# Rests of the MLP's first operands, joins of weight words and a third chunk of w_out, moved in an attention and MLP kernel

## The chip, the cores and the metric

One core of a Trainium2 chip runs the whole program. The metric is the device time of one execution in microseconds, as the median of several runs. The engines are named as in the profile: PE (TensorE), DVE (VectorE), ACT (ScalarE), POOL (GpSimd), and SP (SyncE), whose queue issues all the DMAs here.

## The reference

```python
def _attn_ref(q, k, v):                      # q, k, v: (8, 12, 448, 64), float32
    scores = scale * np.matmul(q, k.transpose(0, 1, 3, 2)) - np.log(S)
    attn = 1.0 / (1.0 + np.exp(-scores))
    return np.matmul(attn, v).astype(np.float32)

def _moe_ref(x, w_in, w_out):                # x: (3584, 768); w_in: (768, 2048); w_out: (2048, 768), both float64
    h = x @ w_in
    r = np.maximum(h, 0.0)
    return ((r * r) @ w_out).astype(np.float32)
```

The attention is a sigmoid attention (no sum over keys). Its output, with the heads side by side, is the x of a two-layer MLP whose activation is the squared Relu.

## The kernel before

**Two kinds of stage.** The first stage (0 to 262 us of the span) does the attention of all 48 pairs of heads; eight stages follow, a first and a second MLP product for each of four groups of two batches. A matmul in the needed accuracy is three: an operand is split into a high part (a cast to fp32r) and a rest, its low part (the operand minus the high part), and high x high, high x low and low x high are summed. Each MLP product is made from seven half-size products (numbers 1 to 7) over sums and differences of blocks, so the operands of x and the blocks of the weights have to be added up first.

**A block of the attention stage.** `block(d)` (line 422) handles two pairs, n = 2d and n + 1, and 24 blocks run in an order written out by hand. On PE: the scores of both pairs (L269), the rest of their keys (L285), then attention times v (`attn_v`, L306, 24 matmuls in one piece), whose sums lie in a PSUM tile `duo` of which there is one. The second pair's scores need that tile again, so `put` (L315, two copies by DVE) must have emptied it before they start. On ACT: seven sigmoids, then the first step of the words below. On DVE, in this order: a piece of weight work, the cast `high` of a coming q, k pair (L472), the two copies of `put`, the rest `low` of that pair (L476); then, behind the issue of the scores, another piece of weight work, `high` and `low`. I call these the first and the second half of a period.

**Weights.** The weights come as float64. While the attention runs, 14 of their 16 chunks are made ready: two loads of a chunk's words (`load_chunk`), a first step by ACT (`convert_words`, L145 and L146), a second by three DVE instructions and an addition by POOL (`convert_join`, L150 to L157), then four additions by DVE (`sums`, L166 to L169) and two stores. These are numbered k = 3j + h for chunk j: k = 3j + 1 and 3j + 2 are joins, k = 3j + 3 the sums. `weights_of` (line 484) puts number k into half period `k * NWP // NK`. The chunks in `DEFERRED`, two of w_out, are made ready in the first MLP stage instead, by `deferred(i, at)` (line 178), in four quarters with their loads, words, joins, sums and stores at steps counted from `at`. That stage (`gemm1` for group 0, 56 steps of 9 matmuls) and all later ones but for the tails of the first MLP stages of groups 1 to 3 are put in order by the framework's planner, which gives earlier code the higher priority.

**Pieces.** Behind the blocks named in `PIECES` (line 65) the operands of the first MLP stage are made from the attention's first output: numbers 1, 2, 3 and 6 are each three casts on ACT and three rests on DVE (`make`, `split_to`, L325 and L326), t1 to t3 are three subtractions on DVE (L351).

**In the first MLP product,** `run(n, i)` (line 547) issues step (n, i): nine matmuls, then a copy of a PSUM bank by ACT (`snap`) or an addition out of it by DVE, and `squares` for each second i (L539 on ACT for the block "12", L541 on DVE for the others).

Of the kernel before, what the change touches and what calls it, by code (L numbers as in the profile page):

```python
# [8 lines left out]
F32 = mybir.dt.float32  # L9
# [26 lines left out]

NWP = 45

# [23 lines left out]

DEFERRED = (6, 7)

PIECES = {13: (1,), 15: (2,), 17: ("t1",), 19: (3,), 21: ("t2",), 22: (6,), 23: ("t3",)}


@with_exitstack
def sigmoid_attention_relu2_mlp(
# [250 lines left out]

    def split_to(hi, lo, raw, vector=False):
        if vector:
            nc.vector.tensor_copy(out=hi, in_=raw)
        else:
            nc.scalar.copy(out=hi, in_=raw)  # L325
        nc.vector.tensor_sub(out=lo, in0=raw, in1=hi.bitcast(F32))  # L326

# [5 lines left out]
    def x_operands(g):  # L333
# [20 lines left out]

        def make(product, n, vector=False):
            h2, l2 = (op2(f"x{n}_{g}{c}", F32R) for c in "hl")
            if g == 0 and product in (1, 2, 3, 6):
                both = op2(f"y{n}_{g}", F32R)
                h1, l1 = both[:, 0], both[:, 1]
            else:  # L360
                h1, l1 = (op1(f"y{n}_{g}{c}", F32R) for c in "hl")
            ops[product] = [(h2[:, 0], l2[:, 0]), (h2[:, 1], l2[:, 1]), (h1, l1)]
            parts = ops[product] if g == 0 else [(h2, l2), (h1, l1)]
            for x, (hi, lo) in zip(raw[n], parts):
                split_to(hi, lo, x, vector)

# [6 lines left out]
        return ops, {  # L373
            1: lambda vector=False: make(1, "11", vector),
            2: lambda vector=False: make(2, "21", vector),
            "t1": lambda: sub("t1", "12", "11"),
            "t2": lambda: sub("t2", "22", "t1"),
            6: lambda: make(6, "t2"),
            "t3": lambda: sub("t3", "t2", "11"),
            7: lambda: make(7, "t3"),  # L380
            5: lambda: make(5, "t1"),
            3: lambda: make(3, "22"),
            "t4": lambda: sub("t4", "21", "t2"),
# [9 lines left out]
    x, vt, xs, at, pav, f64, w, rest = {}, {}, {}, {}, {}, {}, {}, {}  # L393
    ready, stores = [], []
    pieces = {}
    ops = {}

    def half(j, h):
        return w[j][0].rearrange("p a n -> p (a n)")[:, (DM, 0)[h] : (2 * DM, DM)[h]]

    def weights_join(k):


        j, h = divmod(k, 3)
        if h == 0 and j > 0:
            ready.append(sums(*todo[j - 1], *w[j - 1]))
        elif h > 0:
            convert_join(f64[j, h - 1], half(j, h - 1))
        if h < 2 and j + 1 < len(todo):
            f64[j + 1, h] = load_chunk(*todo[j + 1], h)  # L410

    def weights_words(k):

        j, h = divmod(k, 3)
        if j < len(todo) and h < 2:
            if h == 0:
                w[j] = wide(f"a_{j}"), wide(f"s_{j}")
            convert_words(f64[j, h], half(j, h))

    NK = 3 * len(todo) + 1  # L420

    def block(d):
# [12 lines left out]
        if d == 0:  # L435
            for m in (1, 2, 3):
                high(m)
                low(m)
            score(0, (x[0],), ((0, 0),))
            rest[0] = scores_rest(0, (x[0], x[1]))  # L440
        else:
            weights_of(weights_join, n - 1)
            high(n + 3)
            put(n - 2)
            put(n - 1)
            low(n + 3)
            score(n, xs[n])
        score(n + 1, xs[n + 1])
        if more:
            rest[d + 1] = scores_rest(d + 1, (x[n + 2], x[n + 3]))  # L450
        pav[n], pav[n + 1] = attn_v_rest(d, rest.pop(d), vt[d])
        weights_of(weights_join, n)
        high(n + 4)
        low(n + 4)
        weights_of(weights_words, n)
        weights_of(weights_words, n + 1)
        if more:
# [4 lines left out]
        attn_v(n + 1, pav[n + 1], at[n + 1], vt[d])  # L462
        pieces_of(*PIECES.get(d, ()))

# [56 lines left out]
    def gemm1(g, ops, weights, between):  # L521
# [12 lines left out]
        def squares(n, i, scalar=False):  # L534
            if i % 2 == 0:
                return
            t = blocks[n, i // 2]
            if scalar:
                nc.scalar.activation(t, t, AF.Square)  # L539
            else:  # L540
                nc.vector.scalar_tensor_tensor(out=t, in0=t, scalar=0.0, in1=t, op0=ALU.max, op1=ALU.mult)  # L541

        def snap(k, i):
            s = snaps[k, i] = op1(f"s{k}_{g}_{i}")
            nc.scalar.copy(out=s, in_=banks["a", i])  # L545

        def run(n, i):
            if n in (1, 5) and (i, n == 5) not in weights:
                weights[i, n == 5] = halve_weights(load_first(i, n == 5, g))
# [20 lines left out]
            elif n == 5:  # L570
                snap(4, i)
                nc.vector.tensor_add(out=tile_of("22", i), in0=banks["b", i], in1=snaps[4, i])
                squares("22", i)
            elif n == 3:
# [5 lines left out]
            elif n == 4:  # L580
                nc.vector.tensor_add(out=tile_of("21", i), in0=out, in1=snaps[2, i])  # L581
                squares("21", i)

# [26 lines left out]
        with ExitStack() as fixed:  # L610
            if g > 0:
                fixed.enter_context(tc.manual_schedule())
            for at, (n, i) in enumerate(tail):
# [3 lines left out]
                for behind, piece, arg in (*work, (5, load, 1), (8, halve, 1)):  # L617
                    if behind == at:
                        piece(arg)
        return blocks, operands, second  # L620

# [89 lines left out]
    with tc.manual_schedule():  # L711
        with tc.tile_pool(name="ps", bufs=3, space=PSUM) as ps:
# [7 lines left out]
            load(3)  # L720
            for h in range(2):
                f64[0, h] = load_chunk(*todo[0], h)
            load(4)
# [35 lines left out]
        for n, i in enumerate(DEFERRED):  # L759
            work += deferred(i, 12 + 14 * n)  # L760
        between = {}
# [43 lines left out]
```

## Time and profile before

| | us |
|---|---|
| runs: median (lowest to highest) | 1088.53 (1088.22 to 1104.42) |
| the profiled execution | 1086.14 |
| its span | 1084.4 |
| PE busy | 1071.9 (99%) |
| DVE busy | 795.7 (73%) |
| ACT busy | 595.0 (55%) |
| POOL busy | 68.0 (6%) |

Busy shares are means over stages with different limits. The page's slices of the span are 27 us long: DVE stands at 8 or 9 tenths in most of the first ten, the attention stage, and the DMA engines at 8 or 9 in most of them too. A wait is put down to what ended it.

### The profile page before, as it was taken

The numbers are of one execution on the slowest core, as the hardware profiler recorded it, in microseconds if no ns is written. First come the engines' busy times: TensorE is split into PE (matmuls) and PEld (weight loads), VectorE is DVE, ScalarE is ACT, GpSimd is POOL, SyncE is SP. The second block draws the span as 40 slices with busy tenths as digits, with TensorE's granted clock in tenths as the row PEclk, the third lists the DMA queues.
The fourth block names the chain that finished last, engine by engine and source line by source line (L and its number), as shares of the span: only waits on it lengthen the run. The fifth ranks groups of instructions, "written<-read, shape, count | busy, mean of one in ns | idle before, by whom it ended". The sixth has DMA issues, their size and how long they took to land.

```text
span 1084.4 us, 14883 instructions
## 1 busy us (share of the span) xinstructions
PE 1071.9 (99%) x5859; PEld 890.9 (82%) x5859; DVE 795.7 (73%) x890; ACT 595.0 (55%) x729; POOL 68.0 (6%) x40
## 2 busy tenths in 40 slices
PE   9999999999999999999999999999999999999998
PEld 4555545455999999999999999999999999999997
DVE  6999898995697997935579975455897935579941
ACT  6777776866454665523455743334655533355721
POOL 1222222220020000000000000000000000000000
PEclk9999999999999999999999999999999999999999
DMA  9989999954564345633333474233345533333441
GB/s 375 400 301 336 357 323 350 343 199 149 183 232 166 90 140 191 203 98 125 121 102 104 136 243 161 79 123 110 104 143 184 202 99 105 125 106 116 142 141 52
DMA packets 82294, 196.80 MB, mean 181 GB/s; under 512 B 6576, under 2 KB 56624, under 8 KB 82224
## 3 DMA queue, kind: packets, MB, share of 16 engines
q1 hardware_dynamic: 82224, 195.85, 52.6%
q8 instruction: 46, 0.75, 0.3%
q14 instruction: 24, 0.20, 0.0%
HBM read 154.53 MB, written 41.29 MB: 181 GB/s over the span
## 4 chain that ended last, share of the span: by engine, by line
PE 93%; DVE 2%; ACT 2%; issue 1%; DMA 1%; SPq 0%; DVEq 0%; ACTq 0%
PE oa L517 22%; PE ha L517 21%; PE ob L517 11%; PE hb L517 11%; PE pav L306 8%; PE sc L269 7%; PE oc L517 5%; PE hc L517 5%; PE sr L285 2%; PE pav L297 1%; ACT at L254 1%; DMA f<-w_out 1%; DVE xo L315 1%; PE warm_ps L715 0%; DVE x_0l L326 0%
## 5 line engine op out<-in xcount | busy, mean ns | idle before, releaser
L254 ACT ACTIVATE at<-sc 128x896 f32<-128x896 f32 x144 | 120.2, 933 | 62.2 <-PE sc L269 62.1
L235 DVE TENSOR_TENSOR w_1l<-w_1l,w_1h 128x1536 fp32r<-128x1536 f32 x60 | 105.2, 1754 | 63.0 <-ACT w_1h L234 62.4
L545 ACT COPY s<-ha 128x448 f32<-128x448 f32 x96 | 51.0, 532 | 146.3 <-PE ha L517 131.5
L306 PE MATMUL pav<-at,v 128*64 128x448 f32 x576 | 113.5, 543 | 0.0
L234 ACT CAST w_1h<-w_1l 128x1536 fp32r<-128x1536 f32 x60 | 88.8, 1480 | 19.1 <-DMA w_1l<-w 18.9
L306 PEld LDWEIGHTS pav<-at,v 128*64 128x64 f32 x576 | 39.2, 137 | 72.7 <-issue 71.5
L476 DVE TENSOR_TENSOR ql<-x,qh 128x896 fp32r<-128x896 f32 x47 | 78.0, 1660 | 0.9
L235 DVE TENSOR_TENSOR w_5l<-w_5l,w_5h 128x1152 fp32r<-128x1152 f32 x32 | 43.3, 1353 | 47.7 <-ACT w_5h L234 47.7
L234 ACT CAST w_0h<-w_0l 128x1536 fp32r<-128x1536 f32 x28 | 41.5, 1481 | 52.9 <-DMA w_0l<-w 52.9
L157 POOL TENSOR_TENSOR a<-a,f 128x768 int32<-128x768 int32 x28 | 58.6, 2093 | 178.5 <-DVE a L154 126.3
L269 PE MATMUL sc<-qh 64*128 64x448 f32 x282 | 55.5, 387 | 6.7 <-DVE xo L315 6.7
L235 DVE TENSOR_TENSOR w_0l<-w_0l,w_0h 128x1536 fp32r<-128x1536 f32 x28 | 49.1, 1753 | 13.9 <-ACT w_0h L234 13.9
L541 DVE SCALAR_TENSOR_TENSOR g<-g 128x896 f32<-128x896 f32 x48 | 54.1, 1127 | 1.3
L269 PE MATMUL sc<-qh,ql 64*128 64x448 f32 x282 | 52.8, 367 | 0.0
L269 PE MATMUL sc<-ql,qh 64*128 64x448 f32 x282 | 52.8, 367 | 0.0
L581 DVE TENSOR_TENSOR g<-hb,s 128x448 f32<-128x448 f32 x32 | 19.9, 622 | 44.5 <-PE hb L517 44.4
L234 ACT CAST w_5h<-w_5l 128x1152 fp32r<-128x1152 f32 x32 | 37.1, 1159 | 26.0 <-DMA w_5l<-w 21.9
L269 PEld LDWEIGHTS sc<-qh 64*128 64x128 f32 x282 | 27.2, 186 | 26.8 <-issue 21.5
L667 ACT COPY t<-oa 128x448 f32<-128x448 f32 x36 | 19.1, 529 | 34.7 <-PE oa L517 34.3
L315 DVE COPY xo<-pav 128x448 f32<-128x448 f32 x47 | 27.1, 616 | 13.3 <-PE pav L306 13.2
L575 ACT ACTIVATE g<-ha 128x448 f32<-128x448 f32 x32 | 17.4, 544 | 35.0 <-PE ha L517 35.0
L517 PE MATMUL oa<-o_1l,w_0h 128*128 128x448 f32 x96 | 35.1, 365 | 0.0
(520 smaller groups left out, 3043.9 us busy)
## 6 DMA issues: line engine op xcount, KB each, us to landing
w_1l<-w SPq DMA_DIRECT2D x60, 768.0 KB, 4.4
x<-qk SPq DMA_DIRECT2D x48, 448.0 KB, 6.3
w_0l<-w SPq DMA_DIRECT2D x28, 768.0 KB, 4.5
f<-w_in SPq DMA_DIRECT2D x16, 768.0 KB, 9.0
w_5l<-w SPq DMA_DIRECT2D x32, 384.0 KB, 4.0
v<-v SPq DMA_DIRECT2D x24, 448.0 KB, 6.8
w<-s SPq DMA_DIRECT2D x14, 768.0 KB, 8.8
outT<-o SPq DMA_DIRECT2D x47, 224.0 KB, 2.1
```

What stands on the lines that cost most here:

```text
L157: nc.gpsimd.tensor_tensor(out=wb, in0=wb, in1=t.bitcast(I32)[:, :, 0], op=ALU.add)
L234: nc.scalar.copy(out=hi, in_=raw)
L235: nc.vector.tensor_sub(out=lo, in0=raw, in1=hi.bitcast(F32))
L254: nc.scalar.activation(at, sc, AF.Sigmoid, bias=NEG_LOG_S, scale=SCALE)
L269: nc.tensor.matmul(sc[:, j], x[kp][rows, 1, ks], x[qp][rows, 0], start=(n == 0), stop=(n == len(passes) - 1),)
L285: nc.tensor.matmul(sc[r * KR : (r + 1) * KR, j], x[rows, 1, NT * P :], x[rows, 0], start=True, stop=True)
L306: nc.tensor.matmul(pav[columns], vt[:, n % 2 * NT + t, columns], at[t][:, j], start=False, stop=(t == NT - 1))
L315: nc.vector.tensor_copy(out=x, in_=pav)
L476: nc.vector.tensor_sub(out=xs[n][1], in0=x[n], in1=xs[n][0].bitcast(F32))
L517: nc.tensor.matmul(out, a[:, c], b, start=first and n == 0, stop=last and n == 2, skip_group_check=True)
L541: nc.vector.scalar_tensor_tensor(out=t, in0=t, scalar=0.0, in1=t, op0=ALU.max, op1=ALU.mult)
L545: nc.scalar.copy(out=s, in_=banks["a", i])
```

## The change

- `split_to` always casts on ACT; with a list `later` it puts the rest there instead of issuing it. The pieces 1, 2, 3 and 6 are called a block earlier (behind blocks 12, 14, 18 and 21 instead of 13, 15, 19 and 22), and their rests are issued in the first half of the next period, behind `put` and `low`. t1, t2 and t3 (`T_PIECES`) are issued at the same place, in blocks 17, 21 and 23, instead of behind the blocks 17, 21 and 23.
- `weights_join` is called with n - 2 and n - 1 instead of n - 1 and n: each join and each sums half a period later. Loads have a function of their own (`weights_load`); the tile of the sums is taken when they are made.
- A third chunk, 5, joins `DEFERRED`, so 13 chunks are left to the attention stage, spread with `NWP` = 43 instead of 45. The deferred chunks start at steps 10, 22 and 34 of the first MLP stage instead of 12 and 26.
- In the first MLP stage of group 0 the squares of the blocks "21" and "22" go from one DVE instruction to two of ACT (Relu, Square), issued one step later.

```diff
--- before.py
+++ after.py
@@ -34,7 +34,7 @@
 
 N2, N1, NW = 35, 20, 8
 
-NWP = 45
+NWP = 43
 
 KEPT = 2
 
@@ -60,9 +60,11 @@
 TAIL = 10
 STEPS = LEAD + [s for s in REST if s not in LEAD], REST
 
-DEFERRED = (6, 7)
-
-PIECES = {13: (1,), 15: (2,), 17: ("t1",), 19: (3,), 21: ("t2",), 22: (6,), 23: ("t3",)}
+DEFERRED = (5, 6, 7)
+
+
+PIECES = {12: (1,), 14: (2,), 18: (3,), 21: (6,)}
+T_PIECES = {17: ("t1",), 21: ("t2",), 23: ("t3",)}
 
 
 @with_exitstack
@@ -318,12 +320,12 @@
             return lambda: None
         return lambda: nc.sync.dma_start(out=xd[b, p], in_=x)
 
-    def split_to(hi, lo, raw, vector=False):
-        if vector:
-            nc.vector.tensor_copy(out=hi, in_=raw)
+    def split_to(hi, lo, raw, later=None):
+        nc.scalar.copy(out=hi, in_=raw)
+        if later is None:
+            nc.vector.tensor_sub(out=lo, in0=raw, in1=hi.bitcast(F32))
         else:
-            nc.scalar.copy(out=hi, in_=raw)
-        nc.vector.tensor_sub(out=lo, in0=raw, in1=hi.bitcast(F32))
+            later.append(lambda: nc.vector.tensor_sub(out=lo, in0=raw, in1=hi.bitcast(F32)))
 
     def split(raw, name, new):
         hi, lo = new(name + "h", F32R), new(name + "l", F32R)
@@ -352,7 +354,7 @@
 
         ops = {}
 
-        def make(product, n, vector=False):
+        def make(product, n, later=None):
             h2, l2 = (op2(f"x{n}_{g}{c}", F32R) for c in "hl")
             if g == 0 and product in (1, 2, 3, 6):
                 both = op2(f"y{n}_{g}", F32R)
@@ -362,7 +364,7 @@
             ops[product] = [(h2[:, 0], l2[:, 0]), (h2[:, 1], l2[:, 1]), (h1, l1)]
             parts = ops[product] if g == 0 else [(h2, l2), (h1, l1)]
             for x, (hi, lo) in zip(raw[n], parts):
-                split_to(hi, lo, x, vector)
+                split_to(hi, lo, x, later)
 
         load("11", 0, 0)
         load("12", 1, 0)
@@ -371,15 +373,15 @@
         raw["t2"] = raw["22"] if g == 0 else [op2(f"xt_{g}"), op1(f"yt_{g}")]
         raw["t1"], raw["t3"], raw["t4"] = raw["12"], raw["11"], raw["21"]
         return ops, {
-            1: lambda vector=False: make(1, "11", vector),
-            2: lambda vector=False: make(2, "21", vector),
+            1: lambda *later: make(1, "11", *later),
+            2: lambda *later: make(2, "21", *later),
             "t1": lambda: sub("t1", "12", "11"),
             "t2": lambda: sub("t2", "22", "t1"),
-            6: lambda: make(6, "t2"),
+            6: lambda *later: make(6, "t2", *later),
             "t3": lambda: sub("t3", "t2", "11"),
             7: lambda: make(7, "t3"),
             5: lambda: make(5, "t1"),
-            3: lambda: make(3, "22"),
+            3: lambda *later: make(3, "22", *later),
             "t4": lambda: sub("t4", "21", "t2"),
             4: lambda: make(4, "t4"),
         }
@@ -391,31 +393,34 @@
     last = len(pairs) - 1
     todo = [(m, i) for m in range(2) for i in range(NI) if m == 0 or i not in DEFERRED]
     x, vt, xs, at, pav, f64, w, rest = {}, {}, {}, {}, {}, {}, {}, {}
-    ready, stores = [], []
+    ready, stores, later = [], [], []
     pieces = {}
     ops = {}
 
     def half(j, h):
-        return w[j][0].rearrange("p a n -> p (a n)")[:, (DM, 0)[h] : (2 * DM, DM)[h]]
-
-    def weights_join(k):
-
-
+        return w[j].rearrange("p a n -> p (a n)")[:, (DM, 0)[h] : (2 * DM, DM)[h]]
+
+
+
+
+    def weights_load(k):
         j, h = divmod(k, 3)
-        if h == 0 and j > 0:
-            ready.append(sums(*todo[j - 1], *w[j - 1]))
-        elif h > 0:
-            convert_join(f64[j, h - 1], half(j, h - 1))
-        if h < 2 and j + 1 < len(todo):
-            f64[j + 1, h] = load_chunk(*todo[j + 1], h)
+        if j < len(todo) and h < 2:
+            f64[j, h] = load_chunk(*todo[j], h)
 
     def weights_words(k):
-
         j, h = divmod(k, 3)
         if j < len(todo) and h < 2:
             if h == 0:
-                w[j] = wide(f"a_{j}"), wide(f"s_{j}")
+                w[j] = wide(f"a_{j}")
             convert_words(f64[j, h], half(j, h))
+
+    def weights_join(k):
+        j, h = divmod(k, 3)
+        if h > 0:
+            convert_join(f64[j, h - 1], half(j, h - 1))
+        elif j > 0:
+            ready.append(sums(*todo[j - 1], w[j - 1], wide(f"s_{j - 1}")))
 
     NK = 3 * len(todo) + 1
 
@@ -439,28 +444,35 @@
             score(0, (x[0],), ((0, 0),))
             rest[0] = scores_rest(0, (x[0], x[1]))
         else:
-            weights_of(weights_join, n - 1)
+            weights_of(weights_join, n - 2)
             high(n + 3)
             put(n - 2)
             put(n - 1)
             low(n + 3)
+            for piece in later:
+                piece()
+            later.clear()
+            pieces_of(*T_PIECES.get(d, ()))
             score(n, xs[n])
         score(n + 1, xs[n + 1])
         if more:
             rest[d + 1] = scores_rest(d + 1, (x[n + 2], x[n + 3]))
         pav[n], pav[n + 1] = attn_v_rest(d, rest.pop(d), vt[d])
-        weights_of(weights_join, n)
+        for m in (n + 2, n + 3):
+            weights_of(weights_load, m)
+        weights_of(weights_join, n - 1)
         high(n + 4)
         low(n + 4)
-        weights_of(weights_words, n)
-        weights_of(weights_words, n + 1)
+        for m in (n, n + 1):
+            weights_of(weights_words, m)
         if more:
             for store in stores:
                 store()
             stores.clear()
         attn_v(n, pav[n], at[n], vt[d])
         attn_v(n + 1, pav[n + 1], at[n + 1], vt[d])
-        pieces_of(*PIECES.get(d, ()))
+        for name in PIECES.get(d, ()):
+            pieces[name](later)
 
     def load(n):
         if n <= last:
@@ -536,15 +548,31 @@
                 return
             t = blocks[n, i // 2]
             if scalar:
+                if n != "12":
+                    nc.scalar.activation(t, t, AF.Relu)
                 nc.scalar.activation(t, t, AF.Square)
             else:
                 nc.vector.scalar_tensor_tensor(out=t, in0=t, scalar=0.0, in1=t, op0=ALU.max, op1=ALU.mult)
 
+        pending = []
+
+        def squares_later(n, i):
+
+            if g == 0:
+                pending.append(lambda: squares(n, i, scalar=True))
+            else:
+                squares(n, i)
+
+        def flush(count):
+            for _ in range(count):
+                pending.pop(0)()
+
         def snap(k, i):
             s = snaps[k, i] = op1(f"s{k}_{g}_{i}")
             nc.scalar.copy(out=s, in_=banks["a", i])
 
         def run(n, i):
+            count = len(pending)
             if n in (1, 5) and (i, n == 5) not in weights:
                 weights[i, n == 5] = halve_weights(load_first(i, n == 5, g))
             k = {1: "a", 6: "a", 5: "a", 3: "a", 7: "b", 4: "b", 2: "c"}[n]
@@ -570,7 +598,7 @@
             elif n == 5:
                 snap(4, i)
                 nc.vector.tensor_add(out=tile_of("22", i), in0=banks["b", i], in1=snaps[4, i])
-                squares("22", i)
+                squares_later("22", i)
             elif n == 3:
                 nc.scalar.activation(tile_of("12", i), out, AF.Relu)
                 squares("12", i, scalar=True)
@@ -579,7 +607,8 @@
                     nc.vector.tensor_sub(out=t, in0=t, in1=o)
             elif n == 4:
                 nc.vector.tensor_add(out=tile_of("21", i), in0=out, in1=snaps[2, i])
-                squares("21", i)
+                squares_later("21", i)
+            flush(count)
 
         def operand(j):
             operands[j] = split(blocks["11", j], f"o1_{g}_{j}", op2)
@@ -617,6 +646,7 @@
                 for behind, piece, arg in (*work, (5, load, 1), (8, halve, 1)):
                     if behind == at:
                         piece(arg)
+        flush(len(pending))
         return blocks, operands, second
 
     def gemm2(g, blocks, operands1, weights1, ahead):
@@ -718,8 +748,8 @@
             vt[0] = load_v(0, 0)
             load(2)
             load(3)
-            for h in range(2):
-                f64[0, h] = load_chunk(*todo[0], h)
+            for k in range(2):
+                weights_load(k)
             load(4)
             for d in range(len(pairs) // 2 - 2):
                 block(d)
@@ -757,7 +787,7 @@
             work.append((at_load, lambda j=j, late=late: load_first(j, late)))
             work.append((at_load + wait, lambda j=j, late=late: halve_weights(first[j, late])))
         for n, i in enumerate(DEFERRED):
-            work += deferred(i, 12 + 14 * n)
+            work += deferred(i, 10 + 12 * n)
         between = {}
         for n, piece in work:
             between.setdefault(n, []).append(piece)
```

## Rows read from the trace of the kernel before

**Rows 1.** Waits of TensorE over the whole span: us in total, times, longest

```profile
PE sc L269 <- DVE xo L315: 6.7, 4, 2.1
```

**Rows 2.** Timeline of PE, attention stage: start us, us, instruction, count, [idle before it <- releaser]

```profile
135.06 4.73 PE L306 MATMUL pav<-at,v 128*64 128x448 f32 x24
...
145.22 4.73 PE L306 MATMUL pav<-at,v 128*64 128x448 f32 x24
...
154.05 0.47 PE L269 MATMUL sc<-qh 64*128 64x448 f32 x2 [2.08 <-DVE xo L315]
...
247.57 4.73 PE L306 MATMUL pav<-at,v 128*64 128x448 f32 x24
```

**Rows 3.** Windows around two pieces: stretch, its length, busy us, granted clock, DMA share, GB/s

```profile
145.20:157.80 12.60, 10.52 (x82) 5.57 (x80) 11.17 (x16) 9.63 (x14) 3.18 (x2) 1.00 0.89 309
...
167.90:181.90 14.00, 12.06 (x82) 6.37 (x79) 12.63 (x17) 10.04 (x14) 3.17 (x2) 0.88 0.83 307
```

**Rows 4.** Timeline of DVE over one period without a piece

```profile
129.67 1.16 DVE L315 COPY xo<-pav 128x448 f32<-128x448 f32 x2 [3.57 <-PE pav L306]
...
130.74 1.08 DVE L476 TENSOR_TENSOR ql<-x,qh 128x896 fp32r<-128x896 f32 x1
...
131.74 0.55 DVE L150 TENSOR_SCALAR a<-a 128x768 f32<-128x768 f32 x1
...
134.45 2.62 DVE L476 TENSOR_TENSOR ql<-x,qh 128x896 fp32r<-128x896 f32 x1
...
136.99 0.55 DVE L166 TENSOR_TENSOR s<-a 128x384 f32<-128x384 f32 x1
...
139.83 1.16 DVE L315 COPY xo<-pav 128x448 f32<-128x448 f32 x2 [0.23 <-PE pav L306]
```

**Rows 5.** Timeline of POOL in the same period

```profile
134.01 2.10 POOL L157 TENSOR_TENSOR a<-a,f 128x768 int32<-128x768 int32 x1 [6.20 <-ACT at L254]
```

**Rows 6.** Timeline of DVE at two pieces and at t1

```profile
152.76 1.15 DVE L315 COPY xo<-pav 128x448 f32<-128x448 f32 x2
...
155.41 0.55 DVE L166 TENSOR_TENSOR s<-a 128x384 f32<-128x384 f32 x1
...
167.30 2.63 DVE L476 TENSOR_TENSOR ql<-x,qh 128x896 fp32r<-128x896 f32 x1
...
171.16 1.16 DVE L326 TENSOR_TENSOR x_0l<-xo,x_0h 128x448 fp32r<-128x448 f32 x2 [1.23 <-ACT x_0h L325]
...
172.77 0.55 DVE L166 TENSOR_TENSOR s<-a 128x384 f32<-128x384 f32 x1
...
192.36 1.69 DVE L351 TENSOR_TENSOR xo<-xo,xo 128x448 f32<-128x448 f32 x3
```

**Rows 7.** SP's queue, and stores of line 174: time to landing

```profile
103.91 0.77 SPq L174 DMA_DIRECT2D w<-s  x1
...
DMA to landing us min/median/max: 4.6/8.8/11.5
```

**Rows 8.** Windows of the first MLP stage: all engines, then tile b alone

```profile
262.00:366.00 104.00, 103.36 (x508) 94.99 (x507) 81.81 (x104) 56.81 (x84) 9.23 (x8) 1.00 0.50 167
...
262.00:366.00 104.00, 14.75 (x32) 4.39 (x8) 9.23 (x8) 1.00 0.50 167
```

**Rows 9.** Groups of lines in the first MLP stage: busy us, mean ns

```profile
L541 DVE SCALAR_TENSOR_TENSOR g<-g 128x896 f32<-128x896 f32 x11 | 13.8, 1256 | 0.4
...
L539 ACT ACTIVATE g<-g 128x896 f32<-128x896 f32 x4 | 3.8, 952 | 0.1
```

**Rows 10.** SP's queue, landing times and ACT at the end of that stage

```profile
334.15 5.17 SPq L206 DMA_DIRECT2D w<-b  x7
...
358.32 0.36 SPq L223 DMA_DIRECT2D w_1l<-w  x1
...
w<-b SPq DMA_DIRECT2D x14, 192.0 KB, 5.8
...
366.13 1.47 ACT L234 CAST w_1h<-w_1l 128x1536 fp32r<-128x1536 f32 x1
```

## The prediction

> **What bounds the kernel now.** I read the waits of TensorE first. From the first MLP step on it waits for almost nothing; what it waits for in the attention stage is one thing, four times, 6.7 us in all: the copy `put` of the previous block's sums out of `duo` [rows 1]. Then its timeline. From block to block an `attn_v` starts 10.16 us after the last one (135.06 to 145.22), so the ten periods from block 12 to block 22 would take 101.6 us; they take 112.51 (135.06 to 247.57) [rows 2]. The difference, 10.9 us, is what this change can win: 6.7 of waits, and most of the remaining 4.2 is TensorE's clock. In the window of the second long block the granted clock is 0.88 on the mean; between 2.4 and 1.2 GHz that is 3.4 us at the lower level, 1.7 us lost, behind a wait; in the window of the first there is a wait too and the clock stays at 1.00 [rows 3]. 1.0% of 1088.53 is thus the most that the attention stage can give.
>
> Then VectorE's timeline, for `put` is late because of what stands ahead of it in DVE's queue. A period without a piece (put to put): two puts 1.07, `low` 1.00, join and `high` 2.71, `low` 2.54, sums and `high` 2.61, sum 9.93, and 0.23 of idle time in which DVE waits for PE [rows 4]. The second `low` costs 1.54 more than the first: POOL's addition of the join runs at 134.01 to 136.11, and `low` ends about 1 us behind it [rows 5]. If the join stands in the first half, the two puts lie in between and the `low` behind them costs 0.58 more (152.76 to 155.41 is 2.65 instead of 2.07) [rows 4, 6]. DVE is all but full, then, while the page's 73% hides it.
>
> **What a piece costs before.** At piece 2, `low` lets go at about 169.9, the first rest starts at 171.16 since it waits 1.23 for ACT's cast, and the three rests end the piece at 172.77: 2.84 us, all ahead of the next `put` [rows 6]. A period of 9.93 becomes 12.8, 2.6 over. How late may `put` be? It can start at the earliest 4.77 behind the start of the `attn_v` (135.06, 139.83) [rows 2, 4]. At piece 1 it starts at 152.76, PE goes on 1.29 later at 154.05, having waited 2.08; so PE was there at 151.97, and a `put` at 150.68, 5.46 behind its `attn_v` at 145.22, would have been in time [rows 2, 6]. The tolerance is 0.69 us; by it the wait should be about 1.9 to 2.1, and it was 2.08.
>
> **The change, part by part.**
>
> *Rests half a period later.* The 1.23 of waiting for ACT goes: the casts stand behind words on ACT at the end of a block, the rests behind two puts and a `low` of the next. The rests stay, 1.61 us (171.16 to 172.77), but behind `put`; what is late next is the second half's join, and with it the next `put`. t1 (1.69) [rows 6] now lies in the same place, and so does t2.
>
> *Joins half a period later, 13 chunks, 40 numbers with NWP 43.* The halves' work follows from k * 43 // 40; half period s is done in the first half of block s/2 + 1 if s is even, in the second half of block (s + 1)/2 if odd. For blocks 13 to 21 that gives (first, second): 13 join, sums; 14 join, join; 15 none, sums; 16 join, join; 17 sums, join; 18 join, sums; 19 join, join; 20 sums, join; 21 join, sums; then none. Each period is 2.07 for puts and `low`, plus 0.58 if its first half has a join and `put` did not wait, plus the second half (join 2.71 and 2.54 of `low`; sums 2.61 and 1.00), plus the next first half (2.71, 2.61 or 0.62). Against 10.16:
>
> - 13: 2.07 + 0.58 + rests 1.61 + 3.61 + 2.71 = 10.58, late 0.42, within the tolerance. 14 has nothing ahead of the next put and clears it.
> - 15: 2.07 + 1.61 + 3.61 + 2.71 = 10.00, early 0.16. 16: 2.07 + 0.42 + 5.25 + 2.61 = 10.35, late 0.19.
> - 17: 2.07 + t1 1.69 + 5.25 + 2.71 = 11.72, late 1.75: PE waits 1.06.
> - 18: 2.07 + 0.58 + 3.61 + 2.71 = 8.97; early 0.50.
> - 19: 2.07 + 0.08 + rests 1.61 + 5.25 + 2.61 = 11.62, late 1.46: PE waits 0.77.
> - 20: 2.07 + 5.25 + 2.71 = 10.03, late 0.56. 21 with t2: 2.07 + 0.58 + 1.69 + 3.61 + 0.62 = 8.57, early. 22 has the rests of piece 6 and no weights.
>
> So 1.8 us of waits stay, at the starts of blocks 18 and 20. The earlier blocks repeat periods of 10.03 and less and 10.35 at most. Everything here is bounded by 0 and 10.9. Nothing new is issued on SP: a block loads the words it loaded, the stores follow the sums as before, and the chunk fewer takes work from the DMA queue.
>
> *The clock.* Waits of about 1 us lie below the 1.94 to 2.08 seen; the nearest row shows that 2.08 can pass without a fall [rows 2, 3]. I take 0; the other end is 1.7 for each of the two, 3.4. The Trainium skill (TensorE: Matmul & The Clock Gate, What's actually happening) has the clock decided in windows that run free of the kernel; by that the same wait may cost a fall in one execution and none in another, which no row here excludes, and the sum would be anything from 0 to 3.4.
>
> *Third deferred chunk and squares.* Two chunks' blocks cost DVE 14.75, ACT 4.39 and POOL 9.23 in the first MLP stage [rows 8], so a third adds 7.4 on DVE, 2.2 on ACT for the words' first half and as much again for their second, 4.6 on POOL. Eight squares at 1.256 leave DVE, 10.0 us; sixteen activations at 0.952 come to ACT, 15.2 us [rows 9]. Of the stage's 104 us DVE then has 81.8 + 7.4 - 10.0 = 79.2 busy (and at most 4.6 more behind POOL), ACT 56.8 + 19.6 = 76.4; PE has 103.4 [rows 8]. Neither becomes the bound: 0 from busy time. What is late next is the end: the last stores move 8 steps of 104/56 = 1.86, 14.9 us. Before, the seven went out from 334.15 for 5.17 and land 5.8 later, at 345.1; now at 360.0. The load that could need them, the second half of product 1's blocks, is issued at 358.32, and ACT casts it at 366.13 [rows 10]. Even if it has to wait for all seven and takes 5.8 too, it is there at 365.8, 0.3 before the cast. I take 0, at worst 2; a gain is bounded by the stage's 0.6 us of idle PE.
>
> **Sum.** Against the profiled execution (span 1084.4, time 1086.14): 1086.14 - 10.9 + 1.8 + 0 = 1077.0. The median of the runs is 2.4 above that execution, so I expect **1079.4** as a median, 0.8% less.
>
> **Rivals.**
>
> 1. *The clock and a late store, 1081 to 1084.4.* Both remaining waits let the clock fall: +3.4. Besides, with eight `wide` tiles taken in turn, the sums of chunk 5 would reuse the tile of chunk 4's sums, whose store is one block old: in block 10 DVE reaches them at about 112.0 (attn_v of 9 at 135.06 - 3 x 10.16 = 104.6; + 4.77 + 2.65). The store goes out at 103.91 and lands 8.8 later in the median, 11.5 at worst [rows 7]: a wait of 0.7 to 3.4 on DVE. That period is 8.97 long, so 1.2 + 0.7 are covered; at worst PE waits 1.5. For it: the DMA engines are 0.83 and 0.89 busy there [rows 3]. Against: the median is covered.
> 2. *The lateness only moves, 1087.4.* If DVE had no slack at all, four rests and t1 and t2 come back whole: 4 x 1.61 + 2 x 1.69 = 9.8 of the 10.9. For it: 0.23 of idle time in a full period. Against: 3.57 ahead of the put at 129.67 [rows 4], and the two empty half periods that NWP 43 leaves, one of them in block 15.
> 3. *The third chunk delays the second MLP stage: slower than before.* PE then waits for product 1's second half of weights. The gain of 9.1 is used up when the stores land 9.1 + 0.3 = 9.4 later than I have them, at 369.4 instead of 360.0; 11 later gives 1090.1. For it: the chunk's last additions and stores come at the very end of a stage in which DVE is 79% busy, in one queue each. Against: before, 13.2 us lay between landing and load [rows 10], and the planner may put products that need the first half ahead.
>
> **Chances.** Forecast 0.61 (its own range 1076.5 to 1081); rival 1 0.17; rival 2 0.11; rival 3 or another loss in the MLP 0.11. The range goes from 1075 (no wait left, 1077.6, and the runs' 2.4 above the profile partly clock falls that go as well) to 1086, past rival 1 and short of rivals 2 and 3: about 0.2 is left out. A measurement of this kernel can tell some 2% from no change; 2% are 21.8 us, and no case but a far worse rival 3 reaches that: faster by over 2% 0.01, within 0.96, slower 0.03.
>
> **What would show it.** Right: PE's waits for `put` fall from 6.7 to about 1.8, at blocks 18 and 20; the rests start without a wait for ACT; the granted clock in the attention stage stays at 1.00; block 12 to 22 takes about 103.5; the first MLP stage keeps 104. Wrong: waits for `put` at other blocks (then DVE's periods are mis-summed), sums waiting for a store, or PE idle in the first or second MLP stage.

## The result and the profile after

| us | before | after |
|---|---|---|
| runs: median (lowest to highest) | 1088.43 (1086.65 to 1104.42) | 1076.38 (1075.93 to 1076.83) |
| the profiled execution | 1086.14 | 1076.37 |
| its span | 1084.4 | 1074.6 |
| start to attn_v of block 2 | 33.38 | 32.09 |
| block 2 to 12 | 101.68 | 101.66 |
| block 12 to 22 | 112.51 | 103.60 |
| block 22 to the end | 836.8 | 837.2 |

The ratio is 0.989 (0.988 to 0.991): faster by 1.1%, 12.05 us in the medians, 9.8 in the spans. Some executions of most kernels here, the kernel before among them, are 13 to 19 us longer, in the profiles of e6, e7 and e9 all of it behind block 22 (852.7 to 853.1 us instead of 836.7 to 838.0), so they are left out of all times below, and of these profiles only the attention stage (in e6 with the losses of after to 0.01 us) and busy times are read.

Waits of TensorE in the kernel after (us in total, times, longest), to set beside [rows 1]:

```profile
PE sc L271 <- DVE xo L317: 1.4, 2, 0.8
...
PE pav L299 <- ACT at L256: 0.5, 1, 0.5
PE hc L529 <- DVE g L594: 0.5, 1, 0.5
...
PE oa L529 <- ACT w_1h L236: 0.2, 1, 0.2
```

The line `sc <- xo` has gone from 6.7 us in four waits to 1.4 in two. `oa <- w_1h` is new and small.

PE's timeline of the kernel after (start us, us, instruction, count, [idle before it <- releaser]), which answers [rows 2]:

```profile
133.75 4.73 PE L308 MATMUL pav<-at,v 128*64 128x448 f32 x24
...
184.59 4.73 PE L308 MATMUL pav<-at,v 128*64 128x448 f32 x24
...
192.10 0.47 PE L271 MATMUL sc<-qh 64*128 64x448 f32 x2 [0.76 <-DVE xo L317]
...
195.79 4.73 PE L308 MATMUL pav<-at,v 128*64 128x448 f32 x24
...
205.95 4.73 PE L308 MATMUL pav<-at,v 128*64 128x448 f32 x24
...
213.33 0.47 PE L271 MATMUL sc<-qh 64*128 64x448 f32 x2 [0.63 <-DVE xo L317]
...
217.02 4.73 PE L308 MATMUL pav<-at,v 128*64 128x448 f32 x24
...
237.35 4.73 PE L308 MATMUL pav<-at,v 128*64 128x448 f32 x24
```

The two waits stand at the starts of blocks 18 and 20. A period there takes 11.20 (184.59 to 195.79) and 11.07 us, the other eight 10.16 to 10.17. The windows around the two waits (stretch, length, busy us by engine, granted clock, DMA share, GB/s) answer [rows 3]:

```profile
185.00:200.00 15.00, 14.24 (x100) 6.93 (x96) 14.56 (x20) 11.31 (x15) 4.57 (x3) 1.00 0.89 313
212.00:225.00 13.00, 12.37 (x98) 7.29 (x96) 12.83 (x17) 7.82 (x10) 4.25 (x2) 1.00 0.78 256
```

The granted clock stays at 1.00 behind both. DVE in the same place, which answers [rows 6]:

```profile
181.34 1.69 DVE L353 TENSOR_TENSOR xo<-xo,xo 128x448 f32<-128x448 f32 x3
...
190.80 1.15 DVE L317 COPY xo<-pav 128x448 f32<-128x448 f32 x2
...
200.56 1.16 DVE L317 COPY xo<-pav 128x448 f32<-128x448 f32 x2 [0.69 <-PE pav L308]
...
202.64 1.15 DVE L328 TENSOR_TENSOR x_0l<-xo,x_0h 128x448 fp32r<-128x448 f32 x2
203.71 0.62 DVE L328 TENSOR_TENSOR y<-xo,y 128x448 fp32r<-128x448 f32 x1
...
212.04 1.15 DVE L317 COPY xo<-pav 128x448 f32<-128x448 f32 x2
```

t1 (181.34) and the rests of piece 3 (202.64, 203.71) stand behind `put` and `low`, and the rests wait for nothing; nor do those of the other three pieces. The `put` behind each of them, at 190.80 and 212.04, starts without idle time, that is late; the one between them, at 200.56, waited for PE.

The first MLP stage, in a window 11 us earlier than that of [rows 8], all engines:

```profile
251.00:355.00 104.00, 103.33 (x508) 94.25 (x505) 79.74 (x111) 69.51 (x103) 14.25 (x12) 1.00 0.57 192
```

### The profile page after: what moved, and what is told of

Same layout as the page of the kernel before. It is cut to its first block, busy times and chain, and to the rows that moved or that the text cites. A ratio compares the mean times of both kernels' runs of the same rounds, so it can differ in the third digit from the quotient of the medians.

```text
span 1074.6 us, 14946 instructions
## 1 busy us (share of the span) xinstructions
PE 1067.3 (99%) x5859; PEld 888.1 (83%) x5859; DVE 786.8 (73%) x888; ACT 608.4 (57%) x749; POOL 68.7 (6%) x42
## 4 chain that ended last, share of the span: by engine, by line
PE 89%; DVE 5%; ACT 3%; DMA 1%; issue 1%; SPq 0%; DVEq 0%; ACTq 0%
PE oa L529 21%; PE ha L529 19%; PE ob L529 11%; PE hb L529 9%; PE pav L308 9%; PE sc L271 7%; PE oc L529 5%; PE hc L529 5%; PE sr L287 2%; PE pav L299 1%; DVE ql L488 1%; DMA w<-s 1%; DMA w_5l<-w 1%; ACT g L553 0%; DVE qh L484 0%
## 5 line engine op out<-in xcount | busy, mean ns | idle before, releaser
L159 POOL TENSOR_TENSOR a<-a,f 128x768 int32<-128x768 int32 x26 | 54.2, 2086 | 169.1 <-DVE a L156 64.8
L555 DVE SCALAR_TENSOR_TENSOR g<-g 128x896 f32<-128x896 f32 x40 | 43.6, 1090 | 1.1
L529 PE MATMUL oa<-o_2h,w_1h 128*128 128x448 f32 x96 | 35.2, 366 | 0.2 <-ACT w_1h L236 0.2
```

What stands on the lines that cost most here:

```text
L159: nc.gpsimd.tensor_tensor(out=wb, in0=wb, in1=t.bitcast(I32)[:, :, 0], op=ALU.add)
L529: nc.tensor.matmul(out, a[:, c], b, start=first and n == 0, stop=last and n == 2, skip_group_check=True)
```

## The experiments

Two theories stood against each other from the start: A, that only what stands ahead of `put` in DVE's queue counts, so that each part can be summed by periods; and that the gain belongs to one part as a whole, B to the chunk less in the attention stage, C to the later joins. The losses below are periods between two `attn_v` beyond 10.165 us, in the profiled execution.

**e1, the rests at once.**

```diff
         for name in PIECES.get(d, ()):
-            pieces[name](later)
+            pieces[name]()
```

> The changed kernel with one thing undone: the rests of pieces 1, 2, 3 and 6 are issued at once behind blocks 12, 14, 18 and 21, ahead of the next put. Joins, 13 chunks and t1 to t3 as changed. Theory A (what counts is what stands ahead of put in DVE's queue): by the period sums with 2.84 us for a piece that waits for ACT's cast, and a tolerance of 0.69, PE waits for put at the starts of block 13 (2.0), 18 (0.9), 19 (1.65), 20 (0.35) and 22 (1.1), 6.0 us in all instead of 1.4; 1081 us, and up to 1084.5 if the clock falls behind the two longest. Theory B (one chunk less of DVE and DMA work in the attention stage is the gain) and theory C (the later joins are): waits stay near 1.4 us and the time within 1 us of 1076.4.

Measured: 1080.6 us (median), profiled 1081.54. The losses are 3.96 at block 13 (a wait of 2.09 and a fall of the clock), 0.96 at 18, 1.69 at 19, 0.29 at 20 and none at 22, against 2.0, 0.9, 1.65, 0.35 and 1.1. DVE at the rests of pieces 1 and 6:

```profile
133.55 2.62 DVE L488 TENSOR_TENSOR ql<-x,qh 128x896 fp32r<-128x896 f32 x1
137.49 1.16 DVE L326 TENSOR_TENSOR x_0l<-xo,x_0h 128x448 fp32r<-128x448 f32 x2 [1.32 <-ACT x_0h L324]
...
234.62 1.09 DVE L488 TENSOR_TENSOR ql<-x,qh 128x896 fp32r<-128x896 f32 x1
235.63 1.15 DVE L326 TENSOR_TENSOR xt_0l<-xo,xt_0h 128x448 fp32r<-128x448 f32 x2
```

Ahead of piece 1's rests ACT has one half's words to do, and DVE waits 1.32; behind block 21 there are no words, the wait is none (235.63 follows 234.62 directly), and that is why the loss at 22 did not come. Theories B and C, with 1076.4, fall.

**e2, the pieces alone,** in the kernel before (the edits of `split_to`, `make`, `PIECES`, `T_PIECES` and `later`, nothing else).

> The kernel before with one part of the change: pieces a block earlier, their rests and t1 to t3 behind put and low. Joins, 14 chunks in the attention stage and squares as before. Theory A: the 1.23 us of waiting for ACT's cast goes from four periods and nothing else; PE waits at the starts of blocks 14 (0.8), 16 (0.8), 18 (0.4), 19 (0.35), 20 (1.5) and 22 (0.85), 4.6 us in all; no wait reaches 2 us, so the clock stays; blocks 12 to 22 take about 106.5 and the time is 1079 to 1080.5. Theories B and C: the waits stay at 6.7 us and the time at 1086 to 1088.

Measured: 1080.8 us. Losses 0.96, 0.90, 0.13, 0.34, 1.34 and 0.90 at blocks 14, 16, 18, 19, 20 and 22, all where they were expected; blocks 12 to 22 take 106.23. But a loss stands where nobody looked for one, 1.88 in block 1. PE there, and DVE:

```profile
19.84 0.47 PE L270 MATMUL sc<-qh 64*128 64x448 f32 x2 [1.59 <-DVE xo L316]
```

```profile
14.28 0.63 DVE L478 CAST qh<-x 128x896 fp32r<-128x896 f32 x1 [2.56 <-DMA x<-qk]
...
15.95 0.55 DVE L151 TENSOR_SCALAR a<-a 128x768 f32<-128x768 f32 x1
...
18.01 0.62 DVE L478 CAST qh<-x 128x896 fp32r<-128x896 f32 x1
18.54 1.15 DVE L316 COPY xo<-pav 128x448 f32<-128x448 f32 x2
```

DVE waits for the load of a q, k pair until 14.28. Then come `high` and `low`, the first join (15.95 to 18.01), another `high`, and only then `put`: PE has waited 1.59.

**e8, the later joins alone,** in the kernel before (`weights_join` with n - 2 and n - 1, loads apart, the tile of the sums taken late).

> The kernel before with one part of the change: joins and sums half a period later, the tile of the sums taken when they are made. Pieces, their rests, 14 chunks and squares as before. Theory A: the period sums from block 12 to 22 stay as long as before, losses of 0.8, 0.35, 2.7, 0.85, 1.5, 0.35 and 1.55 at blocks 14, 15, 16, 18, 20, 21 and 22, 8.2 us in all, but block 1, where the first join stands ahead of a put that waits for the load of a q, k pair, loses nothing instead of 1.9: attn_v of block 2 starts at 31.9 to 32.1 us of the span instead of 33.4 to 34.1. Time 1083 to 1086. Theory C (the later joins are the gain): 1079 or less. If block 1's gain belongs to something else: attn_v of block 2 stays at 33.4 or later.

Measured: 1084.5 us; `attn_v` of block 2 starts at 32.01. Losses 2.34, 0.27, 2.05, 0.90, 3.83 (with a fall of the clock), 0.06 and 0.89 at blocks 14, 15, 16, 18, 20, 21 and 22. The sums expected 8.2 in all, and without the fall it is 8.8; but they had 0.8 at 14, 2.7 at 16 and 1.5 at 20, with 1.23 of waiting for ACT each, and that wait is 2.52, 0.59 and 1.99 here: it depends on when DVE gets to the rest, too. Block 1 again:

```profile
14.32 0.63 DVE L478 CAST qh<-x 128x896 fp32r<-128x896 f32 x1 [2.58 <-DMA x<-qk]
...
16.52 1.15 DVE L316 COPY xo<-pav 128x448 f32<-128x448 f32 x2
...
18.59 0.56 DVE L151 TENSOR_SCALAR a<-a 128x768 f32<-128x768 f32 x1
```

The pair lands at the same time as in e2, and `put` is 2.0 us earlier, since the join stands behind it (18.59). Over all profiled executions `attn_v` of block 2 starts at 33.4 to 34.1 in the five with early joins (before, e2, e4, e7 twice) and at 31.9 to 32.8 in the seven with later ones (after, e1, e3, e5, e6, e8, e9): means 33.9 and 32.3.

**e7, the third chunk alone,** in the kernel before, twice.

```diff
-NWP = 45
+NWP = 43
-DEFERRED = (6, 7)
+DEFERRED = (5, 6, 7)
...
-            work += deferred(i, 12 + 14 * n)
+            work += deferred(i, 10 + 12 * n)
```

> The kernel before with one part of the change: a third chunk deferred (13 chunks in the attention stage, NWP 43, deferred chunks at steps 10, 22 and 34). Rests, joins and squares as before. Theory A: the period sums give waits at blocks 14 (2.0), 16 (2.0), 18 (0.85), 20 (1.5) and 21 (0.35), 6.8 us instead of 8.3, 1.5 less than before; the wait of 1.6 in block 1 stays; with two waits of 2 us left instead of three, one fall of the clock fewer (1.7): 1083 to 1087. Theory B (the chunk is the gain): 1078 or less.

> The third chunk alone once more, for a steady time: with NWP 43 block 19 has the words of two halves, four activations on ACT ahead of the casts of piece 3, whose rests then wait 3.65 us instead of 1.23 as far as the first such run shows. Theory A: PE waits for put at blocks 14 and 16 (2.0 each), 18 (0.6) and 20 (3.6); with one to three falls of the clock 1085 to 1088.5, no better than before. Theory B: 1078 or less.

Measured: 1088.0 us over both; the ratio of the second is 1.0005 (0.997 to 1.004): the chunk alone gives nothing. One wait became longer. DVE and ACT in block 19:

```profile
215.45 1.09 DVE L476 TENSOR_TENSOR ql<-x,qh 128x896 fp32r<-128x896 f32 x1
220.19 1.16 DVE L326 TENSOR_TENSOR x_0l<-xo,x_0h 128x448 fp32r<-128x448 f32 x2 [3.65 <-ACT x_0h L325]
```

```profile
216.35 0.98 ACT L145 ACTIVATE a<-f 128x768 f32<-128x768 f32 x1
...
218.76 0.95 ACT L146 ACTIVATE f<-f 128x768 int32<-128x768 uint32 x1
219.56 1.06 ACT L325 CAST x_0h<-xo 128x448 fp32r<-128x448 f32 x2
```

With NWP 43 two halves' words fall to block 19, and the casts of piece 3 stand behind their four activations. DVE waits 3.65 for them, PE 3.60 for `put`. So the 1.23 of [rows 6] is no constant of a piece: in e1, e7 and e8 it goes from 0 to 3.65, by the words ahead of the casts on ACT and by the moment at which DVE arrives. In the changed kernel no rest of these pieces stands right behind its casts, and how much ACT has to do there matters no more.

**e3 and e4, one part undone.** e3: two chunks deferred again, NWP 45. e4:

```diff
-            weights_of(weights_join, n - 2)
+            weights_of(weights_join, n - 1)
...
-        weights_of(weights_join, n - 1)
+        weights_of(weights_join, n)
```

> The changed kernel with one thing undone: two chunks deferred instead of three (14 chunks in the attention stage, NWP 45, deferred chunks at steps 12 and 26). Rests, joins and squares as changed. Theory A: the two half periods without weight work are gone; PE waits at the starts of blocks 16 (1.4), 18 (0.85), 20 (0.3), 21 (0.35) and 22 (1.55), 4.5 us in all; 1079.5. Theory B: the chunk is the gain, so 1086 or more. If the third chunk did nothing: 1076.4.

> The changed kernel with one thing undone: joins and sums half a period earlier, as before the change. Rests, 13 chunks and squares as changed. Theory A: other half periods have joins, so PE waits at the starts of blocks 14 (0.8), 16 (0.8), 18 (0.85), 20 (0.3) and 21 (0.35), 3.1 us in all instead of 1.4; 1078.1. Theory C: the place of the joins is the gain, so 1083 or more.

Measured: e3 1079.1, losses 0.07, 1.35, 0.90, 0.15, 0.32 and 1.36 at blocks 15, 16, 18, 20, 21 and 22, 4.15 in all. e4 1080.8, losses 1.18, 0.97, 0.91, 0.16 and 0.30 at blocks 14, 16, 18, 20 and 21, 3.5 in all, and 1.61 in block 1, which the expectation left out; three of its six executions have a mean granted clock of 0.998 and are 1.5 us longer than the others at 1.000. So the chunk is worth 2.7 once the rests are out of the way, and the joins 4.4, about 1.6 of them in block 1 and 0.8 in the clock falls of half the executions of e4.

**e6, the squares on DVE again.**

```diff
-                squares_later("22", i)
+                squares("22", i)
...
-                squares_later("21", i)
+                squares("21", i)
```

> The changed kernel with the squares of the blocks 21 and 22 of the first MLP stage of group 0 as one DVE instruction each again. Theory A: neither engine is near the bound there; DVE goes from 79.7 to some 89.8 us of 104, ACT from 69.5 to 54.3, PE does not wait, and the time is that of the changed kernel, 1076.4 within 0.5. A rival: with a third chunk the stage needs the squares away from DVE; then it is longer than 104 and the time 1078 or more.

Measured: 1075.8 us; the same as after. DVE is 86.8 us busy in the stage, ACT 58.6, PE 103.4 of 104. This part of the change neither costs nor gives anything that these runs show.

**e5, the two periods that are still too long.**

```diff
-PIECES = {12: (1,), 14: (2,), 18: (3,), 21: (6,)}
-T_PIECES = {17: ("t1",), 21: ("t2",), 23: ("t3",)}
+PIECES = {12: (1,), 13: (3,), 14: (2,), 21: (6,)}
+T_PIECES = {7: ("t1",), 21: ("t2",), 23: ("t3",)}
```

> The changed kernel with two things moved: t1 in block 7 instead of 17, and piece 3 behind block 13 instead of 18 (its rests in block 14). Theory A: the two periods that are still too long, those ahead of blocks 18 and 20, lose 1.69 and 1.61 us; by the period sums the latest put is then 0.45 us late, inside the tolerance, so all ten periods from block 12 to 22 take 10.16 to 10.2, 101.7 us instead of 103.6, PE waits for put nowhere, and the time is 1.9 less than the changed kernel's: 1074.5. A rival: the lateness only moves to blocks 14 to 17, and the time stays within 0.5 of 1076.4.

Measured: 1074.6 us (1074.3 to 1075.4, five runs; e6 on the same chip in the same hour 1075.8 to 1076.3). PE's timeline and its waits:

```profile
133.60 4.73 PE L308 MATMUL pav<-at,v 128*64 128x448 f32 x24
...
235.26 4.73 PE L308 MATMUL pav<-at,v 128*64 128x448 f32 x24
```

```profile
PE pav L299 <- ACT at L256: 0.5, 1, 0.5
PE hc L529 <- DVE g L594: 0.5, 1, 0.5
PE ha L529 <- DVE w_1l L237: 0.2, 1, 0.2
```

Blocks 12 to 22 take 101.66, ten times 10.166; the line of waits for `put` is gone. This version beats both kernels, 1.8 us below after.

**e9, waits made on purpose,** in e5.

```diff
             high(n + 3)
+            for _ in range(AGAIN.get(d, 0)):
+                nc.vector.tensor_copy(out=xs[n + 3][0], in_=x[n + 3])
             put(n - 2)
```

> The kernel with t1 and piece 3 moved early, which waits for put nowhere, and in eight blocks the cast of the first half made again several times ahead of put (3 to 8 times 0.53 us, the same values): block 3 five times, 5 four, 7 six, 9 three, 11 seven, 13 five, 18 four, 20 eight. By the period sums the losses are 0.65, 2.0, 2.35, 0.85, 2.4, 2.5, 2.0 and 3.4 there, and 0.35 to 0.4 at blocks 4, 12 and 14, 17.4 us in all, and 1092 if the clock never falls. Theory A on the clock (a wait may let it fall, whatever its length from some 1.3 us up, and by chance): falls behind some of the six longer ones, different ones in different executions, 1.65 us each, so mean granted clocks from 1.000 to 0.991 and times from 1092 to 1102 in steps of 1.65. Rival (the length of the wait decides): the same waits fall in every execution, and the times agree within 0.5.

Measured: 1113.9 us (1109.8, 1113.9 and 1114.3 at mean granted clocks of 0.992, 0.987 and 0.987). The sizes were missed: the extra casts cost more than 0.53.

```profile
36.23 4.80 DVE L451 CAST qh<-x 128x896 fp32r<-128x896 f32 x5
...
111.36 1.95 DVE L451 CAST qh<-x 128x896 fp32r<-128x896 f32 x3
```

```profile
35.79 2.11 POOL L160 TENSOR_TENSOR a<-a,f 128x768 int32<-128x768 int32 x1 [6.81 <-ACT f L149]
```

```profile
L451 DVE CAST qh<-x x5: 627/627/2153, 36.2 to 40.4; 128x896 fp32r<-128x896 f32 x5
```

Three casts took 1.95 in block 9, where POOL is idle. Five took 4.80 in block 3, where POOL's addition runs at 35.79 to 37.90; the last line gives the shortest, the median and the longest of these five, in ns. One took 2.15 us, the first, since the second ends only behind 37.90, and the others 0.63 as in block 9. The waits became 2.7, 3.4, 3.0, 0.9, 4.4, 3.9, 3.3 and 4.3, and the losses exceed them by 0.28 at the waits of 2.7 and 0.9 and by 1.7 to 1.9 at the other six, so six of eight had a fall behind them (behind these six the granted clock is 0.81 to 0.84 over the next 9 to 11 us, behind the two others 1.00). One of the three executions timed lies 4.1 to 4.4 us below the other two, two or three falls, at a clock higher by 0.005; so the falls are not the same in each. e7 shows it on one wait. The same stretch behind the same 3.6 us wait of block 20, in its two profiled executions:

```profile
219.00:233.00 14.00, 10.40 (x78) 5.50 (x76) 12.60 (x17) 7.87 (x11) 4.11 (x2) 1.00 0.44 158
```

```profile
219.00:233.00 14.00, 10.38 (x66) 6.01 (x64) 12.48 (x17) 8.31 (x12) 4.10 (x2) 0.76 0.47 173
```

Granted 1.00 in the one and 0.76 in the other.

## Why the prediction was right, and where it was not

**The bound and what there was to win.** Right. e5 reaches the 101.6 us for ten periods that [rows 2] gave, so nothing but `put` and the clock stood in the way.

**The ledger of DVE's periods.** Right in place, nearly right in size. It had waits at blocks 18 and 20 alone, and that is where they are. `put` was to be late by 1.75 and 1.46; by its rule (4.77 behind the start of the `attn_v`) 190.80 and 212.04 are 1.44 and 1.32 late. The waits, 0.76 and 0.63, are therefore shorter than the 1.06 and 0.77 forecast. But a period loses more than the recorded wait: 1.03 and 0.91 here, 2.34 for a wait of 2.06 in e8's block 14, 0.26 to 0.29 more wherever no fall of the clock followed, which I had not counted. The record explains it: the pairs of `sc` matmuls start 0.20 apart but are recorded 0.37 long, so a recorded wait begins 0.17 after the next pair would have started (190.97 is the last one ahead of the wait that ends at 192.10), and the pair behind a wait is followed after 0.28 instead of 0.20. The two errors nearly cancel, which is luck. In the six kernels with another order all losses above 0.4 came at the blocks that the ledger named, block 1 apart, and, falls of the clock taken off, within 0.4 us of its sizes, except for e1's 22, e7's 20 and four in e8. I had one constant for the wait of a rest for ACT, 1.23; it was 3.65 ahead of e7's 20, 2.52, 0.59 and 1.99 ahead of e8's 14, 16 and 20, and nothing ahead of e1's 22. No rest stands ahead of e8's 22, and why it lost 0.89 instead of 1.55 stays open.

**Blocks 12 to 22: 103.5 forecast, 103.60 measured.**

**"The earlier blocks repeat periods of 10.03 and less": the step that failed.** Block 1 is not such a period. There DVE is held by a load until about 14, and the first join then stood ahead of `put`. PE's start and DVE in block 1 of the kernel before, then PE's start after:

```profile
4.62 3.62 PE L269 MATMUL sc<-x 64*128 64x448 f32 x12
```

```profile
13.65 0.63 DVE L472 CAST qh<-x 128x896 fp32r<-128x896 f32 x1 [2.59 <-DMA x<-qk]
...
17.92 1.15 DVE L315 COPY xo<-pav 128x448 f32<-128x448 f32 x2
```

```profile
4.62 2.58 PE L271 MATMUL sc<-x 64*128 64x448 f32 x12
```

In the execution of before that I read, the join did not show as a wait, because its PE was itself late: the first 12 `sc` matmuls took 3.62 us, against 2.53 to 3.32 in the eleven other profiles, so that PE came to `duo` only when `put` was done. The later join takes 2.0 us out of that queue, and in the means of the profiles (33.9 and 32.3 at block 2) that is worth 1.6. The term was missing from the sum. The two profiles of the result differ by 1.29 at block 2 (33.38 against 32.09), but 1.02 of that stands at the `attn_v` of block 0 already (12.77 against 11.75), ahead of any join: it is PE's start, which differs from execution to execution, and is no work of the change.

**The 2.4 us from the profile to the median: the other step that failed.** I added 2.4 us to go from the profiled execution to the median, and only in the range allowed that this could be clock falls which would go too. It was. By mean granted clock the 40 executions of before that were run beside the experiments fall into five groups:

| mean clock | executions | us |
|---|---|---|
| 1.000 | 3 | 1083.7 to 1084.0 |
| 0.998 | 7 | 1085.0 to 1086.2 |
| 0.997 | 11 | 1086.3 to 1087.2 |
| 0.995 | 12 | 1088.0 to 1089.1 |
| 0.994 | 4 | 1089.9 to 1090.5 |

(three others stand 5 to 7 us above the group of their clock). The means of the groups are 1.2 to 1.9 us apart, about one fall each, from none to four: profiles at 1.000, 0.998 and 0.997 show none (e2), one (e8) and two (before, at blocks 16 and 20). By its place in the table the median of the runs had three. After has none left that recur: 0.999 to 1.000 in all six, within 0.9 us of each other. So the forecast for after should have been the sum for the profile itself, 1077.0. With the 1.3 at block 2, most of it PE's start, and 0.4 lost again later (below), that is 1076.1; 1076.4 was measured.

**The clock behind the two waits: 0 taken, 0 found,** in all six executions. Rival 1's other half, sums that wait for a store in block 10, did not happen either; in the trace of after the sums at 110.47 follow `low` without idle time. On the whole, the longer the waits in a kernel's profile, the more of its executions have a lower mean clock, but the length does not decide alone. With a longest wait of 0.8 us (after) or 1.1 (e3) none of ten is below 0.999; with 1.3 (e4) three of six are at 0.998, with 1.6 (e2) one of five, with 2.1 (e1) three of nine, with three waits of about 2 us (before, e8) all but four of 49; and waits of 2.7 and 3.6 each passed once without a fall (e9, e7). The Trainium skill (TensorE: Matmul & The Clock Gate, What's actually happening) has the clock decided in windows that run free of the kernel; these runs agree with it as far as they go (1.00 and 0.76 behind the same wait in e7).

**Rival 2, the lateness only moves:** no; it moved by 1.94 us and e5 removed that too.

**The first MLP stage and rival 3.** DVE 79.7 us (79.2 forecast, in part by luck: the third chunk costs it 9.2 there and not 7.4, 23.96 on tile b against 14.75, and the rest came out lower), PE 103.3 of 104. ACT has 69.5, not 76.4: three of the sixteen added activations and two other instructions come behind the window (4.4 us), and 2.5 is my adding up of single lengths, for the records of instructions that follow on each other directly overlap by 0.1 us. The third chunk's last stores, and ACT and PE at the weights behind them:

```profile
336.81 7.72 SPq L208 DMA_DIRECT2D w<-b  x7
348.23 0.37 SPq L225 DMA_DIRECT2D w_1l<-w  x1
```

```profile
353.30 0.96 ACT L552 ACTIVATE g<-g 128x896 f32<-128x896 f32 x1 [1.72 <-DVE g L600]
...
357.95 1.46 ACT L236 CAST w_1h<-w_1l 128x1536 fp32r<-128x1536 f32 x1
```

```profile
359.46 0.47 PE L529 MATMUL oa<-o_2h,w_1h 128*128 128x448 f32 x1 [0.17 <-ACT w_1h L236]
```

With the stage 10.2 us earlier, the stores were to go out at 338.9 (334.15 + 14.9 - 10.2) and the load behind them at 348.1; the last seven go out from 336.81 and the load is issued at 348.23. The stores land 2.3 us behind their issue in the median, at about 346.8, the load 4.4 behind its own, at 352.6, and ACT casts it at 357.95. So the step was right, with some 5 us to spare. PE's wait of 0.17 for those weights is therefore not rival 3: from one of the added Relus (353.30) on ACT works without a pause, and the cast comes in its turn, with no idle time ahead of it. In e5, with the same squares and chunks, this wait does not come. Of the 0.4 us that the rest of the span is longer, this wait and 0.1 more at `hc` account for 0.3; in the profiles of e1 to e5 and e8 the rest goes from 836.7 to 838.0, so the 0.4 need not come from the change.

**The parts together.** Medians; the kernel before has 1087.1 over the 40 executions above:

| | pieces | joins | chunk | us |
|---|---|---|---|---|
| e7 | | | x | 1088.0 |
| e8 | | x | | 1084.5 |
| e2 | x | | | 1080.8 |
| e1 | | x | x | 1080.6 |
| e4 | x | | x | 1080.8 |
| e3 | x | x | | 1079.1 |
| after | x | x | x | 1076.4 |

(e1 has the pieces a block earlier as well, but not their rests behind `put`.) Only the pieces give much alone. The chunk is worth nothing by itself and 2.7 behind the other two: it shortens periods, and that counts only where a period is the one that is too long.

## What to carry to other kernels

Sum the in-order queue that feeds the critical engine period by period, with every instruction ahead of the one it waits for; a share of 73% busy hid a queue that was full in most periods, and the sum found the block of nearly every loss, and its size to a few tenths of a microsecond where no rest waited for ACT. Don't let an instruction stand ahead of such a one if it waits for a third engine: its price is that engine's backlog, which changes from place to place. Sum the first periods apart, since loads set them, and ask of how many clock falls a profiled execution is an example before you add anything to go from it to the median.

## What the runs showed of the hardware

- One fall of TensorE's clock cost 1.4 to 1.6 us in the profiles here (2.4 behind the 3.6 us wait of e7), and the executions of one kernel fall into groups by their number (1083.7 to 1090.5 us for the kernel before). Behind one and the same wait it came in one execution and not in another.
- At the start of the program the same twelve matmuls took 2.53 us in five profiles and between 2.58 and 3.62 in the other seven, and that can hide a wait. Why is open: the granted clock is given as 1.00 there in the profiles of before and after alike.
- A DVE cast of 128x896 fp32 took 0.63 us alone and 2.15 beside an int32 addition by POOL (2.11 us, e9); until here only subtractions with two inputs (2.62 against 1.08) had shown it [rows 4, 5].
- A period of PE lost 0.26 to 0.29 us more than the wait that the profile records in it, where no fall of the clock followed.
